# A decode step with attention and a gated FFN: activations as the stationary operand in q projection and FFN up, and w_down in 112 rows

## The chip, the cores and the metric

The kernel runs on one core of a Trainium2 chip. The time is the device time of one execution in microseconds (us). Before the change the runs took 125.03 us in the median (three runs, 124.83 to 125.47). The chip's matrix engine is called PE (its weight loads PEld), the vector engine DVE, the scalar engine ACT, the general engine POOL, and the engine that issues most transfers SP. On PE one operand is loaded first and stays (stationary), the other streams past it (moving).

## The reference, cut to what matters

One token for each of 8 sequences, model width 512, all data bf16.

```python
x  = A_x                                    # 8 x 1 x 512
xn = layernorm(x)
q  = (xn @ wq)                              # 512 x 4096: 32 heads of 128
k, v = last 1024 positions of the caches    # 8 sequences x 8 kv heads x 1024 x 128
o  = softmax(q k^T / sqrt(128)) v           # 4 query heads share a kv head
s  = o @ wo                                 # 4096 x 512
h  = gelu(xn @ w_gate) * (xn @ w_up)        # 512 x 1792 each
g  = silu(h @ w_down)                       # 1792 x 512
out = x + s * g
```

About 47 MB are read: 32 MB of caches (16 groups of K and 16 of V, 1 MB each), wq and wo with 4 MB each, and the three FFN weights with 1.8 MB each. Little is computed per byte.

## The kernel before

**Loads.** Every large load goes into a slot of one ring, `ring`, of 22 slots of 128 partitions x 8192 bytes, and all are issued by SP in one order, written out by hand: K group 0, four parts of wq, then K and V groups in turn (`load_cache`, L86), two halves each of w_gate and w_up (L105) and of w_down (L114), and four parts of wo (L132), the last of which is cut in 768 KB and 256 KB. The transfers are spread over 16 DMA engines. SP holds a load back until the load eight places earlier has landed, and, once the ring has gone round, until PE is done with the slot's last content.

**Start.** The layer norm's result `xhat` (8 x 512) is transposed on PE (L230, L234) into `xnT_sb` and, with another order of rows, `xpT_sb`, 128 x 4 x 8 each. `project_q` has wq as the stationary operand: for each of 4 parts and 32 heads, one matmul with 128 x 128 weights and 8 moving columns (L242). The result has head dimension on partitions, as the scores need it, and one cast (L250) brings it to `qT_all`.

**Attention.** A group is 4 sequences of one kv head. Its K comes as 32 blocks of 128 x 128; PE transposes them eight at a time (L262), DVE copies them to SBUF (L266), and they become the stationary operand of the scores (L274). ACT takes the exponential (L284), a matmul with ones and a DVE reduction give the sums (L296, L298), and V blocks are the stationary operand of the values (L309). The main loop runs over 64 such blocks of eight, transposing two blocks ahead of the scores and multiplying values six blocks behind them. PE runs in program order: what waits there holds up what follows.

**FFN and end.** After the loop, `ffn_up` multiplies 128-column pieces of w_gate and w_up (stationary, read with a step of 7 elements) by `xpT_sb` (8 moving columns, L379): 112 matmuls into one PSUM tile `gu_ps`, with the hidden dimension on partitions. Then come the gelu and the product on ACT and DVE (L389 to L402, 112 elements per partition), which leave `hT_sb`. Between, `select_out` (L350) finishes the rearrangement of the last attention outputs. `ffn_down` (L409) has 8 columns of `hT_sb` stationary and w_down moving, 128 columns at a time, and puts the four quarters of the output at partitions 0, 32, 64 and 96. `project_out` (L363) does the same with wo, part by part as it lands, and two DVE operations and four small stores end the kernel.

```python
load_k(0)
load_wq()
for g in range(1, NG):
    load_k(g)
    load_v(g - 1)
load_v(NG - 1)
load_ffn()
```

Of the kernel before, what the change touches and what calls it, by code (L numbers as in the profile page):

```python
# [8 lines left out]
ALU = mybir.AluOpType  # L9
AX = mybir.AxisListType  # L10
BF16 = mybir.dt.bfloat16
FP32 = mybir.dt.float32
# [3 lines left out]
def kernel(  # L16
# [13 lines left out]
    nc = tc.nc  # L30

    B, Sq, D = A_x.shape
    Hkv, Sk, Dh = A_k_cache.shape[1], A_k_cache.shape[2], A_k_cache.shape[3]
    Hq = A_wq.shape[1] // Dh
    rep = Hq // Hkv
    W = min(4096, max(256, Sk // 4))
    win0 = Sk - W
    F = B_w_gate.shape[1]
    P = nc.NUM_PARTITIONS
    NDC = D // P  # L40
# [11 lines left out]
    NB = C // CB  # L52
    SLOT = C * Dh

    JF = F // 2 // P
    NQ = D // P

    consts = ctx.enter_context(tc.tile_pool(name="consts", bufs=1))
    persist = ctx.enter_context(tc.tile_pool(name="persist", bufs=1))
    ring = ctx.enter_context(tc.tile_pool(name="ring", bufs=22))  # L60
    kT_pool = ctx.enter_context(tc.tile_pool(name="kT_pool", bufs=4))
    p_pool = ctx.enter_context(tc.tile_pool(name="p_pool", bufs=3))
    small = ctx.enter_context(tc.tile_pool(name="small", bufs=3))
# [2 lines left out]
    ps_m = ctx.enter_context(tc.tile_pool(name="ps_m", bufs=2, space=bass.MemoryType.PSUM))  # L66
# [9 lines left out]
    def slot():  # L76
        return ring.tile([P, SLOT], BF16, name="slot")

    k_t, v_t, wo_t = {}, {}, {}
    wq_t, wg_t, wu_t, wd_t = [], [], [], []  # L80
# [20 lines left out]
    def load_ffn():  # L101
        for dst, src in ((wg_t, B_w_gate), (wu_t, B_w_up)):
            for a in range(2):
                t = slot()
                nc.sync.dma_start(  # L105
                    out=t[:, 0 : 2 * F],
                    in_=src[a * 2 * P : (a + 1) * 2 * P, :].rearrange(
                        "(p k) f -> p (k f)", k=2
                    ),
                )  # L110
                dst.append(t[:, 0 : 2 * F].rearrange("p (k f) -> p k f", k=2))
        for a in range(2):
            t = slot()
            nc.sync.dma_start(  # L114
                out=t[:, 0 : JF * D],
                in_=B_w_down[a * JF * P : (a + 1) * JF * P, :].rearrange(
                    "(p j) d -> p (j d)", j=JF
                ),
            )
            wd_t.append(t[:, 0 : JF * D].rearrange("p (j d) -> p j d", j=JF))  # L120


    HS = SLOT // D
# [13 lines left out]
# [5 lines that stand above are left out]
    for m in range(NM):  # L142
        load_wo(m, cut=HS if m < NM - 1 else HS - 2)


    ident = consts.tile([P, P], BF16, name="ident")
    nc.vector.memset(ident, 0.0)
    nc.gpsimd.affine_select(
        out=ident, in_=ident, compare_op=ALU.not_equal, fill=1.0, base=0,
# [10 lines left out]
        out=sel, in_=sel, compare_op=ALU.not_equal, fill=1.0, base=0,  # L160
# [4 lines left out]
        out=diag, in_=sel.rearrange("p r i -> p i r"), axis=AX.X, op=ALU.add  # L165
    )
    nc.vector.tensor_scalar(
        out=diag, in0=diag, scalar1=1.0, scalar2=30000.0, op0=ALU.subtract, op1=ALU.mult
# [6 lines left out]
        out=hmask, in_=hmask, compare_op=ALU.is_ge, fill=0.0, base=0,  # L175
# [3 lines left out]
        out=hmask, in_=hmask, compare_op=ALU.is_ge, fill=0.0, base=B - 1,  # L179
# [5 lines left out]
        out=bsel3, in_=bsel3, compare_op=ALU.not_equal, fill=1.0, base=0,  # L185
# [4 lines left out]
        out=bsel_f, in_=bsel3.rearrange("p h b -> p b h"), axis=AX.X, op=ALU.add  # L190
# [6 lines left out]
    nc.gpsimd.memset(xq_sb, 0.0)  # L197
    for q in range(NQ):
        nc.scalar.dma_start(
            out=xq_sb[32 * q : 32 * q + B, :], in_=x_flat[:, q * P : (q + 1) * P]  # L200
# [12 lines left out]
        out=xhat, in0=x_sb, scalar1=mv[:, 0:1], scalar2=rstd[:, 0:1],  # L213
        op0=ALU.subtract, op1=ALU.mult,
    )

    xnT_sb = persist.tile([P, NDC, B], BF16, name="xnT_sb")
    xpT_sb = persist.tile([P, NDC, B], BF16, name="xpT_sb")
    qT_all = persist.tile([P, Hkv, B, rep], BF16, name="qT_all")
    oT_all = persist.tile([P, Hq, B], BF16, name="oT_all")  # L220
    hT_sb = persist.tile([P, 2 * JF, B], BF16, name="hT_sb")
    g_sb = persist.tile([P, P], FP32, name="g_sb")

    s_ps = ps_s.tile([P, P], FP32, name="s_ps")
# [2 lines left out]
    def transpose_x():  # L227
        t = ps_m.tile([P, 2, NDC, B], BF16, name="m_ps")
        for k in range(NDC):
            nc.tensor.transpose(t[:, 0, k, :], xhat[:, k * P : (k + 1) * P], ident[0:B, 0:B])  # L230
        xp = xhat.rearrange("b (a p k) -> b a k p", a=2, k=2)
        for a in range(2):
            for k in range(2):
                nc.tensor.transpose(t[:, 1, 2 * a + k, :], xp[:, a, k, :], ident[0:B, 0:B])  # L234
        nc.vector.tensor_copy(out=xnT_sb, in_=t[:, 0])
        nc.vector.tensor_copy(out=xpT_sb, in_=t[:, 1])

    def project_q():
        q_ps = ps_m.tile([P, Hq, B], FP32, name="m_ps")
        for k in range(NDC):  # L240
            for h in range(Hq):
                nc.tensor.matmul(  # L242
                    q_ps[:, h, :],
                    wq_t[k][:, h * Dh : (h + 1) * Dh],
                    xnT_sb[:, k, :],
                    start=(k == 0 and h == 0),
                    stop=(k == NDC - 1),
                    skip_group_check=True,
                )
        nc.vector.tensor_copy(  # L250
            out=qT_all, in_=q_ps.rearrange("p (h j) b -> p h b j", j=rep)
        )


    kT, sc, pT, oT = {}, {}, {}, {}
# [104 lines left out]
    def project_out(m):  # L360
        for e in range(HS):
            for q in range(NQ):
                nc.tensor.matmul(  # L363
# [7 lines left out]


    def ffn_up():
        gu_ps = ps_m.tile([P, 2, 2 * JF, B], FP32, name="m_ps")
        for w, wt in enumerate((wg_t, wu_t)):
            for j in range(2 * JF):
                f0 = (j // JF) * (F // 2) + j % JF
                for k in range(NDC):
                    nc.tensor.matmul(  # L379
                        gu_ps[:, w, j, :],  # L380
                        wt[k // 2][:, k % 2, f0 : f0 + (P - 1) * JF + 1 : JF],
                        xpT_sb[:, k, :],
                        start=(k == 0),
                        stop=(k == NDC - 1),
                    )
        shape = [P, 2 * JF, B]
        zT, uT = gu_ps[:, 0], gu_ps[:, 1]
        z2 = persist.tile(shape, FP32, name="z2")
        nc.scalar.activation(out=z2, in_=zT, func=ACT.Square)  # L389
        nc.vector.tensor_scalar(  # L390
            out=z2, in0=z2, scalar1=0.044715, scalar2=1.0, op0=ALU.mult, op1=ALU.add
        )
        u3 = persist.tile(shape, FP32, name="u3")
        nc.vector.tensor_tensor(out=u3, in0=z2, in1=zT, op=ALU.mult)
        th = persist.tile(shape, FP32, name="th")
        nc.scalar.activation(out=th, in_=u3, func=ACT.Tanh, scale=0.7978845608028654)
        nc.vector.tensor_scalar(
            out=th, in0=th, scalar1=0.5, scalar2=0.5, op0=ALU.mult, op1=ALU.add
        )
        gz = persist.tile(shape, FP32, name="gz")  # L400
        nc.vector.tensor_tensor(out=gz, in0=th, in1=zT, op=ALU.mult)
        nc.vector.tensor_tensor(out=hT_sb, in0=gz, in1=uT, op=ALU.mult)  # L402

    def ffn_down():
        f_ps = ps_m.tile([P, P], FP32, name="m_ps")
        nc.vector.memset(f_ps, 0.0)
        for j in range(2 * JF):
            for q in range(NQ):
                nc.tensor.matmul(  # L409
                    f_ps[32 * q : 32 * q + B, :],  # L410
                    hT_sb[:, j, :],
                    wd_t[j // JF][:, j % JF, q * P : (q + 1) * P],
                    start=(j == 0),
                    stop=(j == 2 * JF - 1),
                    skip_group_check=True,
                )
        th2 = persist.tile([P, P], FP32, name="th2")
        nc.scalar.activation(out=th2, in_=f_ps, func=ACT.Tanh, scale=0.5)
        nc.vector.tensor_scalar(
            out=th2, in0=th2, scalar1=0.5, scalar2=0.5, op0=ALU.mult, op1=ALU.add  # L420
        )
        nc.vector.tensor_tensor(out=g_sb, in0=th2, in1=f_ps, op=ALU.mult)


    LA, LAG = 2, 6
    N = NG * NB
    transpose_x()
    for n in range(LA):
        transpose_block(n)
    project_q()  # L430
    for n in range(N + LAG):
        if n + LA < N:
# [3 lines left out]
        if n >= LAG:  # L436
# [3 lines left out]
            if g % GM == 0 and g > 0:  # L440
                if s == 0:
                    expand_out(g // GM - 1)
                if s == 3:
                    select_out(g // GM - 1)
    expand_out(NM - 1)
    ffn_up()
    select_out(NM - 1)
    ffn_down()
# [8 lines left out]
    nc.vector.tensor_tensor(out=out_sb, in0=tmp, in1=xr_sb, op=ALU.add)  # L457
    for q in range(NQ):
        eng = nc.sync if q % 2 == 0 else nc.scalar
        eng.dma_start(  # L460
            out=out_flat[:, q * P : (q + 1) * P], in_=out_sb[32 * q : 32 * q + B, :]
# [31 lines left out]
```

## Time and profile before

| what | value |
|---|---|
| median of the runs | 125.03 us |
| profiled execution, its own time | 124.83 us |
| its span in the profile | 123.1 us |
| PE, PEld busy | 85.5, 79.9 us |
| DVE, ACT, POOL busy | 69.1, 22.0, 2.1 us |
| read from HBM | 47.46 MB, 386 GB/s over the span |
| q projection: matmuls L242 | 128, 4.1 us |
| FFN up: matmuls L379 | 112, 6.5 us |
| FFN down: matmuls L409 | 56, 1.7 us |
| transposes of K, L262 | 512, 45.5 us |

A line of the profile names the source line, the engine, the operation, output and inputs with their shapes, how often it ran and how long. In square brackets or behind a bar stands how long the engine was idle before, and what it waited for. The slices divide the span into 40 equal parts of about 3.1 us; a digit is the busy share in tenths. PEclk is the share of full clock that PE was granted: 0.50 in some stretches, 1.00 in others. The chain that ended last is followed back from the last instruction. The times in a timeline count from the start of the span.

### The profile page before, as it was taken

The numbers are of one execution on the slowest core, as the hardware profiler recorded it, in microseconds if no ns is written. First come the engines' busy times: TensorE is split into PE (matmuls) and PEld (weight loads), VectorE is DVE, ScalarE is ACT, GpSimd is POOL, SyncE is SP. The second block draws the span as 40 slices with busy tenths as digits, with TensorE's granted clock in tenths as the row PEclk, the third lists the DMA queues.
The fourth block names the chain that finished last, engine by engine and source line by source line (L and its number), as shares of the span: only waits on it lengthen the run. The fifth ranks groups of instructions, "written<-read, shape, count | busy, mean of one in ns | idle before, by whom it ended". The sixth has DMA issues, their size and how long they took to land.

```text
span 123.1 us, 4441 instructions
## 1 busy us (share of the span) xinstructions
PE 85.5 (69%) x2020; PEld 79.9 (65%) x2020; DVE 69.1 (56%) x146; ACT 22.0 (18%) x70; POOL 2.1 (2%) x13
## 2 busy tenths in 40 slices
PE   0075339696976968999987982998799756927260
PEld 0075339595865947999976982998699646926240
DVE  2352006775956849579997990769899660052001
ACT  0440000330303302121330330123033300010000
POOL 6000000000000000000000000000000000000000
PEclk9999999999999975559999997569999965556955
DMA  3999999999999999999999999999999999999820
GB/s 88 397 415 434 418 415 423 423 413 421 410 418 415 418 418 413 423 410 421 413 413 418 423 418 418 423 407 415 407 423 410 422 415 412 413 417 426 322 106 5
DMA packets 6931, 47.76 MB, mean 388 GB/s; under 512 B 888, under 2 KB 896, under 8 KB 1920
## 3 DMA queue, kind: packets, MB, share of 16 engines
q1 hardware_dynamic: 6800, 47.46, 93.7%
q8 instruction: 16, 0.26, 0.9%
q10 hardware_dynamic: 112, 0.02, 0.1%
q14 instruction: 3, 0.02, 0.0%
HBM read 47.46 MB, written 0.01 MB: 386 GB/s over the span
## 4 chain that ended last, share of the span: by engine, by line
DMA 88%; PE 5%; SPq 3%; issue 1%; DVE 0%
DMA slot<-in_A_k_cache_dram 50%; DMA slot<-in_B_w_gate_dram 16%; DMA slot<-in_A_wo_dram 15%; DMA slot<-in_A_wq_dram 7%; SPq L86 3%; PE kT_ps L262 3%; PE s_ps L363 1%; PE m_ps L309 1%; PE sc_ps L274 0%; SPq L98 0%; PE m_ps L296 0%; DVE tmp L455 0%; DVE out_sb L457 0%; SPq L132 0%
## 5 line engine op out<-in xcount | busy, mean ns | idle before, releaser
L266 DVE COPY kT<-kT_ps 128x1024 bf16<-128x1024 bf16 x64 | 42.3, 678 | 19.1 <-PE kT_ps L262 18.4
L262 PE MATMUL kT_ps<-ident,slot 128*128 128x128 bf16 x512 | 45.5, 241 | 9.9 <-DMA slot<-in_A_k_cache_dram 9.8
L262 PEld LDWEIGHTS <-slot 128*128 128x128 bf16 x512 | 34.3, 108 | 13.4 <-DMA slot<-in_A_k_cache_dram 10.6
L284 ACT ACTIVATE pT<-sc_ps,diag 128x128 bf16<-128x128 f32 x64 | 18.3, 368 | 71.6 <-PE sc_ps L274 71.6
L274 PE MATMUL sc_ps<-qT_all,kT 128*128 128x16 bf16 x512 | 23.0, 172 | 0.0
L309 PE MATMUL m_ps<-pT,slot 128*128 128x16 bf16 x512 | 21.8, 170 | 0.2 <-issue 0.2
L309 PEld LDWEIGHTS <-slot 128*128 128x128 bf16 x512 | 18.6, 97 | 3.5 <-issue 2.0
L274 PEld LDWEIGHTS <-kT 128*128 128x128 bf16 x512 | 20.8, 100 | 0.0
L298 DVE TENSOR_REDUCE sums<-m_ps 128x16 f32<-128x512 f32 x16 | 10.9, 683 | 1.0 <-PE m_ps L296 1.0
L242 PE MATMUL m_ps<-xnT_sb,slot 128*128 128x8 bf16 x128 | 4.1, 169 | 5.5 <-DMA slot<-in_A_wq_dram 5.5
L379 PE MATMUL m_ps<-xpT_sb,slot 128*128 128x8 bf16 x112 | 6.5, 195 | 2.0 <-DMA slot<-in_B_w_up_dram 1.3
L379 PEld LDWEIGHTS <-slot 128*128 128x128 bf16 x112 | 6.2, 153 | 2.3 <-DMA slot<-in_B_w_up_dram 1.3
L242 PEld LDWEIGHTS <-slot 128*128 128x128 bf16 x128 | 3.9, 105 | 5.7 <-DMA slot<-in_A_wq_dram 5.7
L296 PE MATMUL m_ps<-pT,ones_pp 128*128 128x512 bf16 x16 | 6.7, 416 | 0.7 <-ACT pT L284 0.7
L250 DVE CAST qT_all<-m_ps 128x256 bf16<-128x256 f32 x1 | 0.4, 425 | 8.6 <-PE m_ps L242 8.6
L336 DVE TENSOR_TENSOR wide<-m_ps,hmask 64x1024 bf16<-64x1024 bf16 x4 | 4.9, 1217 | 0.4 <-PE m_ps L332 0.3
L230 PE MATMUL m_ps<-ident,xhat 8*128 8x8 bf16 x4 | 0.3, 168 | 6.9 <-DVE xhat L212 6.9
L230 PEld LDWEIGHTS <-xhat 8*128 8x128 bf16 x4 | 0.2, 104 | 6.9 <-DVE xhat L212 6.9
L390 DVE TENSOR_SCALAR z_2490<-z_2490 128x112 f32<-128x112 f32 x1 | 0.2, 219 | 7.5 <-ACT z_2490 L389 7.5
L302 DVE RECIPROCAL recip<-sums 128x16 f32<-128x16 f32 x16 | 4.0, 253 | 0.5
L455 DVE TENSOR_TENSOR tmp<-s_ps,g_sb 128x128 f32<-128x128 f32 x1 | 0.3, 292 | 6.5 <-PE s_ps L363 6.5
L318 DVE TENSOR_TENSOR oT_all<-m_ps,recip 128x16 bf16<-128x16 f32 x16 | 3.5, 218 | 0.3
(63 smaller groups left out, 28.4 us busy)
## 6 DMA issues: line engine op xcount, KB each, us to landing
slot<-in_A_k_cache_dram SPq DMA_DIRECT2D x16, 1024.0 KB, 19.9
slot<-in_A_v_cache_dram SPq DMA_DIRECT2D x16, 1024.0 KB, 19.9
slot<-in_A_wq_dram SPq DMA_DIRECT2D x4, 1024.0 KB, 8.7
slot<-in_A_wo_dram SPq DMA_DIRECT2D x3, 1024.0 KB, 18.4
slot<-in_B_w_gate_dram SPq DMA_DIRECT2D x2, 896.0 KB, 19.4
slot<-in_B_w_up_dram SPq DMA_DIRECT2D x2, 896.0 KB, 19.0
slot<-in_B_w_down_dram SPq DMA_DIRECT2D x2, 896.0 KB
slot<-in_A_wo_dram SPq DMA_DIRECT2D x1, 768.0 KB, 18.1
```

The costliest lines, as they stand in the source:

```text
L86: nc.sync.dma_start(out=t, in_=rows)
L242: nc.tensor.matmul(q_ps[:, h, :], wq_t[k][:, h * Dh : (h + 1) * Dh], xnT_sb[:, k, :], start=(k == 0 and h == 0), stop=(k == NDC - 1), skip ...
L262: nc.tensor.transpose(t_ps[:, c * P : (c + 1) * P], k_t[g][:, cc * Dh : (cc + 1) * Dh], ident)
L266: nc.vector.tensor_copy(out=kT[n], in_=t_ps)
L274: nc.tensor.matmul(sc[g][:, s * CB + c, :], kT[n][:, c * P : (c + 1) * P], qT_all[:, hkv, b0 : b0 + I, :], start=True, stop=True,)
L284: nc.scalar.activation(out=pT[g][:, :, i * rep : (i + 1) * rep], in_=sc[g][:, :, i * rep : (i + 1) * rep], func=ACT.Exp, bias=diag[:, i : ...
L296: nc.tensor.matmul(sums_ps, ones_pp, pT[g], start=True, stop=True)
L298: nc.vector.tensor_reduce(out=sums, in_=sums_ps.rearrange("p c m -> p m c"), axis=AX.X, op=ALU.add)
L302: nc.vector.reciprocal(out=recip[g], in_=sums)
L309: nc.tensor.matmul(oT[g], v_t[g][:, c * Dh : (c + 1) * Dh], pT[g][:, c, :], start=(c == 0), stop=(c == C - 1),)
L336: nc.vector.tensor_tensor(out=wide, in0=t_ps.rearrange("p (q e) -> p e q", e=HS) .unsqueeze(2) .to_broadcast([HS * B, HS, HS, DQ]), in1=hm ...
L379: nc.tensor.matmul(gu_ps[:, w, j, :], wt[k // 2][:, k % 2, f0 : f0 + (P - 1) * JF + 1 : JF], xpT_sb[:, k, :], start=(k == 0), stop=(k == N ...
```

## The change

Four things change together.

The activations become the stationary operand of the q projection and of FFN up, padded to 32 columns (`xnT_sb` and `xpT_sb` grow to 128 x 4 x 32, zeroed by POOL), and the weights move past them: 512 columns of wq at a time, 448 of w_gate and w_up, the latter with a step of 8 elements. Four such matmuls write to partitions 0, 32, 64 and 96 of one PSUM tile. There are 32 matmuls instead of 128 and 32 instead of 112.

The results then have the sequences on partitions, so they are copied to SBUF and transposed on PE: 8 transposes and four DVE copies for q (in place of one cast), 4 transposes and one copy for the FFN's hidden values. The gelu works on 448 elements per partition instead of 112, and its gate half and up half now lie in separate PSUM tiles.

The hidden dimension is cut in 16 pieces of 112 rows instead of 14 of 128. w_down is loaded in two transfers of 112 partitions x 8192 bytes instead of 128 x 7168, and `ffn_down` does 64 matmuls instead of 56.

The ring has 21 slots instead of 22. The order of the loads is the same; K group 0 is one transfer in both kernels.

```diff
-    JF = F // 2 // P
+    FP = F // 16
+    JF = F // 2 // FP
+    JH = JF // 2
     NQ = D // P
+    Q = 32
-    ring = ctx.enter_context(tc.tile_pool(name="ring", bufs=22))
+    ring = ctx.enter_context(tc.tile_pool(name="ring", bufs=21))
...
-                out=t[:, 0 : JF * D],
-                in_=B_w_down[a * JF * P : (a + 1) * JF * P, :].rearrange(
+                out=t[0:FP, :],
+                in_=B_w_down[a * JF * FP : (a + 1) * JF * FP, :].rearrange(
                     "(p j) d -> p (j d)", j=JF
...
-    xnT_sb = persist.tile([P, NDC, B], BF16, name="xnT_sb")
-    xpT_sb = persist.tile([P, NDC, B], BF16, name="xpT_sb")
+    xnT_sb = persist.tile([P, NDC, Q], BF16, name="xnT_sb")
+    xpT_sb = persist.tile([P, NDC, Q], BF16, name="xpT_sb")
+    nc.gpsimd.memset(xnT_sb, 0.0)
+    nc.gpsimd.memset(xpT_sb, 0.0)
-    hT_sb = persist.tile([P, 2 * JF, B], BF16, name="hT_sb")
+    hT_sb = persist.tile([FP, JH, P], BF16, name="hT_sb")
...
     def project_q():
-        q_ps = ps_m.tile([P, Hq, B], FP32, name="m_ps")
+        NW = rep * Dh
+        q_sb = persist.tile([P, Hkv // NQ, NW], BF16, name="q_sb")
+        q_ps = [ps_m.tile([P, NW], FP32, name="m_ps") for n in range(Hkv // NQ)]
         for k in range(NDC):
-            for h in range(Hq):
+            for hkv in range(Hkv):
+                n, q = hkv // NQ, hkv % NQ
                 nc.tensor.matmul(
-                    q_ps[:, h, :],
-                    wq_t[k][:, h * Dh : (h + 1) * Dh],
+                    q_ps[n][Q * q : Q * (q + 1), :],
                     xnT_sb[:, k, :],
+                    wq_t[k][:, hkv * NW : (hkv + 1) * NW],
...
-        nc.vector.tensor_copy(
-            out=qT_all, in_=q_ps.rearrange("p (h j) b -> p h b j", j=rep)
-        )
+        for n in range(Hkv // NQ):
+            nc.vector.tensor_copy(out=q_sb[:, n, :], in_=q_ps[n])
+        t_ps = ps_m.tile([P, Hkv // NQ, rep, NQ, Q], BF16, name="m_ps")
+        for n in range(Hkv // NQ):
+            for j in range(rep):
+                nc.tensor.transpose(
+                    t_ps[:, n, j].rearrange("p q r -> p (q r)"),
+                    q_sb[:, n, j * Dh : (j + 1) * Dh],
+                    ident,
+                )
+        for n in range(Hkv // NQ):
+            nc.vector.tensor_copy(
+                out=qT_all[:, n * NQ : (n + 1) * NQ],
+                in_=t_ps[:, n, :, :, 0:B].rearrange("p j q b -> p q b j"),
+            )
...
     def ffn_up():
-        gu_ps = ps_m.tile([P, 2, 2 * JF, B], FP32, name="m_ps")
+        gu_ps = [ps_m.tile([P, JH * FP], FP32, name="m_ps") for w in range(2)]
         for w, wt in enumerate((wg_t, wu_t)):
-            for j in range(2 * JF):
-                f0 = (j // JF) * (F // 2) + j % JF
-                for k in range(NDC):
+            for k in range(NDC):
+                for q in range(NQ):
+                    a, j0 = q // 2, JH * (q % 2)
+                    cols = wt[k // 2][:, k % 2, a * JF * FP : (a + 1) * JF * FP]
                     nc.tensor.matmul(
-                        gu_ps[:, w, j, :],
-                        wt[k // 2][:, k % 2, f0 : f0 + (P - 1) * JF + 1 : JF],
+                        gu_ps[w][Q * q : Q * (q + 1), :],
                         xpT_sb[:, k, :],
+                        cols.rearrange("x (p j) -> x j p", j=JF)[:, j0 : j0 + JH, :],
...
-        nc.vector.tensor_tensor(out=hT_sb, in0=gz, in1=uT, op=ALU.mult)
+        h_sb = persist.tile(shape, BF16, name="h_sb")
+        nc.vector.tensor_tensor(out=h_sb, in0=gz, in1=uT, op=ALU.mult)
+        h_ps = ps_m.tile([FP, JH, P], BF16, name="m_ps")
+        for c in range(JH):
+            nc.tensor.transpose(h_ps[:, c, :], h_sb[:, c * FP : (c + 1) * FP], ident)
+        nc.vector.tensor_copy(out=hT_sb, in_=h_ps)
...
         for j in range(2 * JF):
+            r, c = j // JH, j % JH
             for q in range(NQ):
                 nc.tensor.matmul(
-                    f_ps[32 * q : 32 * q + B, :],
-                    hT_sb[:, j, :],
+                    f_ps[Q * q : Q * q + B, :],
+                    hT_sb[:, c, Q * r : Q * r + B],
```

More of the change, by code (lines that the diff above doesn't have):

```diff
@@ L119, in load_ffn @@
             )
-            wd_t.append(t[:, 0 : JF * D].rearrange("p (j d) -> p j d", j=JF))
+            wd_t.append(t[0:FP, :].rearrange("p (j d) -> p j d", j=JF))
     HS = SLOT // D
@@ L234, in transpose_x @@
                 nc.tensor.transpose(t[:, 1, 2 * a + k, :], xp[:, a, k, :], ident[0:B, 0:B])
-        nc.vector.tensor_copy(out=xnT_sb, in_=t[:, 0])
-        nc.vector.tensor_copy(out=xpT_sb, in_=t[:, 1])
+        nc.vector.tensor_copy(out=xnT_sb[:, :, 0:B], in_=t[:, 0])
+        nc.vector.tensor_copy(out=xpT_sb[:, :, 0:B], in_=t[:, 1])
     def project_q():
-        q_ps = ps_m.tile([P, Hq, B], FP32, name="m_ps")
+        NW = rep * Dh
+        q_sb = persist.tile([P, Hkv // NQ, NW], BF16, name="q_sb")
+        q_ps = [ps_m.tile([P, NW], FP32, name="m_ps") for n in range(Hkv // NQ)]
         for k in range(NDC):
-            for h in range(Hq):
+            for hkv in range(Hkv):
+                n, q = hkv // NQ, hkv % NQ
                 nc.tensor.matmul(
-                    q_ps[:, h, :],
-                    wq_t[k][:, h * Dh : (h + 1) * Dh],
+                    q_ps[n][Q * q : Q * (q + 1), :],
                     xnT_sb[:, k, :],
-                    start=(k == 0 and h == 0),
+                    wq_t[k][:, hkv * NW : (hkv + 1) * NW],
+                    start=(k == 0),
                     stop=(k == NDC - 1),
@@ L373, in ffn_up @@
     def ffn_up():
-        gu_ps = ps_m.tile([P, 2, 2 * JF, B], FP32, name="m_ps")
+        gu_ps = [ps_m.tile([P, JH * FP], FP32, name="m_ps") for w in range(2)]
         for w, wt in enumerate((wg_t, wu_t)):
-            for j in range(2 * JF):
-                f0 = (j // JF) * (F // 2) + j % JF
-                for k in range(NDC):
+            for k in range(NDC):
+                for q in range(NQ):
+                    a, j0 = q // 2, JH * (q % 2)
+                    cols = wt[k // 2][:, k % 2, a * JF * FP : (a + 1) * JF * FP]
                     nc.tensor.matmul(
-                        gu_ps[:, w, j, :],
-                        wt[k // 2][:, k % 2, f0 : f0 + (P - 1) * JF + 1 : JF],
+                        gu_ps[w][Q * q : Q * (q + 1), :],
                         xpT_sb[:, k, :],
+                        cols.rearrange("x (p j) -> x j p", j=JF)[:, j0 : j0 + JH, :],
                         start=(k == 0),
                         stop=(k == NDC - 1),
+                        skip_group_check=True,
                     )
-        shape = [P, 2 * JF, B]
-        zT, uT = gu_ps[:, 0], gu_ps[:, 1]
+        shape = [P, JH * FP]
+        zT, uT = gu_ps
         z2 = persist.tile(shape, FP32, name="z2")
```

## The prediction

> **What bounds the kernel now.** I read the page's slices first, then the chain that ended last in order of time, then the timeline of the end, then stretches of one microsecond.
>
> ```profile
> DMA  3999999999999999999999999999999999999820
> GB/s 88 397 415 434 418 415 423 423 413 421 410 418 415 418 418 413 423 410 421 413 413 418 423 418 418 423 407 415 407 423 410 422 415 412 413 417 426 322 106 5
> q1 hardware_dynamic: 6800, 47.46, 93.7%
> q8 instruction: 16, 0.26, 0.9%
> DMA 88%; PE 5%; SPq 3%; issue 1%; DVE 0%
> ```
>
> The 16 DMA engines run without a gap at about 418 GB/s from 3 us on, and 88% of the chain is transfers. So bytes and rate set the time; PE (85.5 of 123.1 us busy) doesn't. The second queue, 16 packets of 16 KB, matters below.
>
> ```profile
> 81.21 19.29 DMA slot<-in_B_w_gate_dram
> ...
> 100.56 18.12 DMA slot<-in_A_wo_dram
> 118.68 0.04 issue
> 118.72 1.07 PE s_ps L363 x32
> 119.78 0.02 issue
> 119.81 0.30 DVE tmp L455
> 120.11 0.02 issue
> 120.13 0.29 DVE out_sb L457
> ```
>
> The last large weight piece lands at 118.68; after it come 32 matmuls, two vector operations and the store. Anything done before 118.68 is free if PE is there in time.
>
> ```profile
> 111.93 1.07 PE L363 MATMUL s_ps<-slot,oE_1142 128*8 128x128 bf16 x32
> 114.30 0.62 PE L363 MATMUL s_ps<-slot,oE_1645 128*8 128x128 bf16 x32 [1.30 <-DMA slot<-in_A_wo_dram]
> 116.81 1.03 PE L363 MATMUL s_ps<-slot,oE_2148 128*8 128x128 bf16 x32 [1.89 <-DMA slot<-in_A_wo_dram]
> 118.72 1.04 PE L363 MATMUL s_ps<-slot,oE_2510 128*8 128x128 bf16 x32 [0.88 <-DMA slot<-in_A_wo_dram]
> ```
>
> PE waits 1.30 + 1.89 + 0.88 = 4.1 us for wo pieces after the FFN, so the FFN has about 4 us of slack. The lines also price column tiles: 32 matmuls of 128 columns in four tiles take 0.62 us at full clock, 19 ns each (77 ns per group of four), and 1.04 us at half clock (130 ns per group).
>
> ```profile
> 115.00:116.00 1.00, 0.00 (x0) 0.00 (x0) 0.00 (x0) 0.00 (x0) 0.00 (x0) 1.00 0.84 326
> 116.00:117.00 1.00, 0.19 (x12) 0.19 (x15) 0.00 (x0) 0.00 (x0) 0.00 (x0) 0.79 0.52 211
> 117.00:118.00 1.00, 0.84 (x32) 0.64 (x25) 0.00 (x0) 0.00 (x0) 0.00 (x0) 0.50 0.47 195
> 118.00:119.00 1.00, 0.28 (x14) 0.28 (x17) 0.00 (x0) 0.00 (x0) 0.00 (x0) 0.50 0.31 115
> ```
>
> The last two numbers are DMA share and GB/s. The engines do not end together: from 115 on they drop out, and the rest work to the end. The landing records (one per engine and load) say the same: the sixteen parts of a wq load arrive within 0.4 us, those of the last 768 KB piece at 115.43 (first) to 118.68 (last), seven of them over 3 us behind. The steps are about 1.6 us each and follow the 16 KB instruction packets: each delays one engine, eight engines take turns, and those with two packets are the 3.2 us late ones. **A load lands with its slowest engine.**
>
> [...] about 4040 PE rows, 16 packets. [...] a packet of 8192 bytes takes 0.313 us, 26.2 GB/s. All large loads of this kernel have 128 rows, so no row here shows 112.
>
> **The change, part by part.**
>
> *q projection.* Before: the last wq part lands at 17.46, 32 matmuls take 1.02 us, one cast 0.43, the first score is at 19.04, 1.6 us after the landing. After, for that part: two groups of four matmuls of 512 columns, 4 x 77 = 0.31 us each. The cast of half 0 can start after the first (0.31); then two casts of 128x512 from PSUM (nearest: the reduction L298 of that size, 683 ns) 1.37; four transposes (eight of L262 take 0.61) 0.3 plus 0.2 for the last to drain; a copy of 128 elements 0.2 (L358: 203 to 225 ns); five handovers of 0.06 to 0.1, 0.35. Sum 2.7 us, so scores start about 1.1 us later. If the four tiles didn't overlap, each matmul would take the 0.22 us from the start of L296 to the next, eight 1.7 us, and the delay would be about 2.5. Behind these instructions on PE stand the transposes of K blocks from the third on, and their copies on DVE; nothing of the DMA: SP's loads do not wait on PE before the ring has gone round, at the 22nd load (about 39.7 us). PE then has 1.35 us idle at 24.8 and 1.2 in each 5 us after, so it is back within two groups. Cost 0; without that cover 1.1 to 2.5. The two POOL memsets (L197: 0.2 us each) end near 3.7, and their readers come at 7.36: 0.
>
> *FFN up.* Before: the second half of w_up is there at 104.94, 54 matmuls take 3.0 us, the gelu chain and waits 2.5, down starts at 110.48 and ends at 112.15. After: 8 matmuls of 448 columns, two groups, half clock: 2 x 3.5 x 130 ns = 0.9 us (with no overlap, at twice 0.22 us and 448/512, 3.1; the moving rows are read with a step of 16 bytes, which no row shows: doubling gives 1.8). The gate half of the gelu runs while w_up arrives; what is left is one product of 128x448, 0.7 us (112 elements 0.27, 128 elements of L455 0.29), four transposes at half clock 0.5, a copy of 512 columns 0.37, then select_out, which now waits for a PSUM buffer of ffn_up, its copy, the memset and handovers, 1.1. Down starts near 108.5, and has 64 instead of 56 matmuls at 30 ns, 1.9 us: 110.4, 1.7 us earlier. With no overlap it is 112.6, still under the 114.30 at which PE goes on. Gain or loss at the end: 0.
>
> *Ring of 21.* A load waits for the PE work on the load 21 before, not 22, i.e. 2.5 us earlier. SP's order is the same, and each load already waits for the landing of the eighth before it (20 us in flight); the slot before was landed some 32 us earlier. 0.
>
> *PE instructions.* 4042 to 3730 rows, 312 fewer, so 14 packets instead of 15 before the last data. Engines with two packets remain, since that is more than eight. Gain 0; it would need another deal of packets to engines to gain up to 1.6.
>
> *w_down in 112 rows of 8192 bytes, not 128 of 7168.* Same bytes, twice 0.92 MB, same bytes per engine (7 x 8192 = 8 x 7168). [...] 7 x 0.313 = 2.19 us per load against 8 x 0.275 = 2.20: 0. [...] The late engines have no reserve, and the two loads stand ahead of wo in every engine's queue, so it goes straight to the end. I take +2.5. What is late next: wo, then the last 32 matmuls.
>
> *Sum.* Span 123.1 + 2.5 = 125.6; the profiled execution took 124.83, 1.7 more than its span, so 127.3; the median of the runs is 0.2 above it: **127.5**.
>
> **Rivals.** (1) *Rows land at full rate whatever their partitions.* Then all parts are hidden and nothing moves: 125.0, from 124.5 to 125.5. [...] It decides if a w_down packet of 8192 bytes stays near 0.31 us; this case ends not slower. [...] (3) *Something gains:* the last matmuls at full clock end at best 0.2 earlier, because the final 256 KB land at 119.33; packets dealt otherwise take off up to 1.6; 123.5 to 124.4. Against: eight turns are seen twice over. (4) *PE becomes the end:* tiles that don't overlap, with doubled reads, make each group of eight 6 us, FFN up 99.5 + 24 = 123.5, and the end about 10 us later, 135. Against: 19 ns per matmul of 128 columns in L363 can't be without overlap.
>
> **How the numbers follow.** [...] No cost: 0.23. Gain: 0.06. Worse than +5 by either road: 0.05. About 0.5% is what a measurement of this kernel can tell from no change. Faster 0.07 (gain and the edge of no cost), same 0.28, slower 0.65. Range 124.7 to 130.0, which leaves out the gain, the worst and the lowest edge of no cost.
>
> **What would show it.** Right: w_down packets of 8192 bytes well over 0.31 us, a dip under 400 GB/s between 96 and 112 us (slices 32 to 37), the final wo landing near 121, q's first score near 20, PE still waiting for wo after an earlier ffn_down. Wrong: GB/s flat at 418 and the last landing at 118.7; or PE busy without a DMA wait at the end.

## The result, and the profile after

The changed kernel takes 129.93 us in the median (129.61 to 130.94) beside 124.97 for the kernel before: a ratio of 1.040, with a 95% interval of 1.034 to 1.047. It is 5.0 us slower. The forecast was 2.5 slower, at 127.5; the direction and the place were right and the size was half. The profiled execution took 130.14 us, with a span of 128.1.

From the page of the changed kernel, the transfers by slice and the two queues:

```profile
DMA  3999999999999999999999999999999999999820
GB/s 120 397 427 412 438 420 438 415 430 422 425 425 417 427 420 435 415 430 420 425 427 417 435 412 432 412 438 417 421 428 422 282 197 220 207 287 436 360 97 5
...
q1 hardware_dynamic: 6768, 47.46, 94.0%
q8 instruction: 14, 0.23, 0.7%
```

For 31 slices the rate is as before or a little higher. Then it falls to about half for five slices (197 to 287 GB/s) while the row above stays at 9: the engines are all busy and move about half as much. There are 14 instruction packets instead of 16.

Stretches of two microseconds over that dip; the last two numbers are DMA share and GB/s:

```profile
98.00:100.00 2.00, 1.91 (x12) 0.70 (x16) 1.25 (x2) 0.00 (x0) 0.00 (x0) 0.50 1.03 432
100.00:102.00 2.00, 2.00 (x16) 0.41 (x12) 0.00 (x0) 0.00 (x0) 0.00 (x0) 0.77 1.15 258
102.00:104.00 2.00, 1.65 (x9) 0.12 (x1) 1.02 (x2) 0.76 (x2) 0.00 (x0) 1.00 1.03 189
...
108.00:110.00 2.00, 1.28 (x16) 0.75 (x12) 0.79 (x2) 0.00 (x0) 0.00 (x0) 0.50 1.06 229
...
114.00:116.00 2.00, 1.02 (x32) 0.83 (x32) 0.00 (x0) 0.20 (x1) 0.00 (x0) 0.50 0.97 401
```

A share of 1.0 at 190 to 260 GB/s means that a packet takes about twice as long, not that engines stand idle. The packet records of the trace agree: from 96 us to the end 378 packets took more than 1.3 times their usual duration (327 of 8192 bytes, 49 of 7168 and two of 6144), most of the 8192-byte ones near 0.6 us instead of 0.31. w_down has 224 packets, all of 8192 bytes. So at least 154 of the slow packets belong to other loads: those of 7168 bytes to w_gate or w_up, and at least 103 of the others to wo. What the slow packets took beyond the usual, added up and divided by the 16 engines, is 7.2 us.

The chain that ended last, its end in order of time:

```profile
...
98.74 24.89 DMA slot<-in_A_wo_dram
123.63 0.04 issue
123.68 1.05 PE s_ps L385 x31
...
```

It still ends with the last large piece of wo and 1.05 us of matmuls; the landing has moved from 118.68 to 123.63. The parts of that piece arrive from 120.35 (first engine) to 123.63 (last), before from 115.43 to 118.68: every engine is 4.9 us later, and the spread of 3.3 us is the same.

PE at the end, from the timeline:

```profile
98.34 5.31 PE L402 MATMUL m_ps<-slot,xpT_sb 128*32 128x448 bf16 x24
106.63 1.77 PE L402 MATMUL m_ps<-slot,xpT_sb 128*32 128x448 bf16 x8 [2.99 <-DMA slot<-in_B_w_up_dram]
...
114.73 1.02 PE L439 MATMUL m_ps<-slot,hT_sb 112*8 112x128 bf16 x32 [2.83 <-DMA slot<-in_B_w_down_dram]
116.98 1.02 PE L385 MATMUL s_ps<-slot,oE_1062 128*8 128x128 bf16 x32 [1.23 <-DMA slot<-in_A_wo_dram]
119.42 1.02 PE L385 MATMUL s_ps<-slot,oE_1565 128*8 128x128 bf16 x32 [1.41 <-DMA slot<-in_A_wo_dram]
121.85 1.03 PE L385 MATMUL s_ps<-slot,oE_2068 128*8 128x128 bf16 x32 [1.41 <-DMA slot<-in_A_wo_dram]
123.68 1.03 PE L385 MATMUL s_ps<-slot,oE_2358 128*8 128x128 bf16 x32 [0.80 <-DMA slot<-in_A_wo_dram]
```

PE waits for w_down (2.83 us) and then for each part of wo, as before: nothing on PE sets the end.

One thing was not forecast. Up to the first half of w_gate the changed kernel runs ahead: the first engine's part of it is there at 93.49 instead of 95.07. From about 4 us up to there a packet of 8192 bytes takes 309 ns almost without exception; in the kernel before it took 313 (most), 316 or 320 from about 12 us on. So the 5.0 us are a loss of nearly 7 less a gain of nearly 2, and both needed an explanation.

### The profile page after: what moved, and what is told of

The parts are those of the page before. It is cut to its first block, busy times and chain, and to the rows that moved or that the text cites. A ratio compares the mean times of both kernels' runs of the same rounds, so it can differ in the third digit from the quotient of the medians.

```text
span 128.1 us, 4139 instructions
## 1 busy us (share of the span) xinstructions
PE 88.0 (69%) x1864; PEld 72.9 (57%) x1864; DVE 72.0 (56%) x150; ACT 22.6 (18%) x70; POOL 2.4 (2%) x15
## 4 chain that ended last, share of the span: by engine, by line
DMA 95%; PE 1%; SPq 1%; DVE 0%; issue 0%
DMA slot<-in_A_k_cache_dram 56%; DMA slot<-in_A_wo_dram 19%; DMA slot<-in_B_w_gate_dram 15%; DMA slot<-in_A_wq_dram 5%; PE s_ps L385 1%; SPq L90 1%; DVE tmp L485 0%; DVE out_sb L487 0%; SPq L136 0%; SPq L109 0%
## 5 line engine op out<-in xcount | busy, mean ns | idle before, releaser
L284 PE MATMUL kT_ps<-ident,slot 128*128 128x128 bf16 x512 | 44.5, 238 | 9.9 <-DMA slot<-in_A_k_cache_dram 9.6
L284 PEld LDWEIGHTS <-slot 128*128 128x128 bf16 x512 | 33.5, 106 | 13.5 <-DMA slot<-in_A_k_cache_dram 10.3
L331 PEld LDWEIGHTS <-slot 128*128 128x128 bf16 x512 | 18.5, 97 | 3.4 <-issue 1.9
L402 PE MATMUL m_ps<-slot,xpT_sb 128*32 128x448 bf16 x32 | 7.1, 971 | 3.0 <-DMA slot<-in_B_w_up_dram 3.0
L252 PE MATMUL m_ps<-slot,xnT_sb 128*32 128x512 bf16 x32 | 4.2, 618 | 3.5 <-DMA slot<-in_A_wq_dram 3.5
L402 PEld LDWEIGHTS <-xpT_sb 128*32 128x32 bf16 x32 | 1.2, 106 | 7.3 <-issue 5.9
L261 DVE CAST q_sb<-m_ps 128x512 bf16<-128x512 f32 x2 | 1.3, 686 | 6.5 <-PE m_ps L252 6.5
L439 PE MATMUL m_ps<-slot,hT_sb 112*8 112x128 bf16 x64 | 2.1, 307 | 3.6 <-DMA slot<-in_B_w_down_dram 3.6
L252 PEld LDWEIGHTS <-xnT_sb 128*32 128x32 bf16 x32 | 1.0, 110 | 6.0 <-issue 5.8
L439 PEld LDWEIGHTS <-hT_sb 112*8 112x8 bf16 x64 | 1.6, 119 | 3.9 <-issue 3.0
```

What stands on the lines that cost most here:

```text
L252: nc.tensor.matmul(q_ps[n][Q * q : Q * (q + 1), :], xnT_sb[:, k, :], wq_t[k][:, hkv * NW : (hkv + 1) * NW], start=(k == 0), stop=(k == NDC ...
L284: nc.tensor.transpose(t_ps[:, c * P : (c + 1) * P], k_t[g][:, cc * Dh : (cc + 1) * Dh], ident)
L331: nc.tensor.matmul(oT[g], v_t[g][:, c * Dh : (c + 1) * Dh], pT[g][:, c, :], start=(c == 0), stop=(c == C - 1),)
L402: nc.tensor.matmul(gu_ps[w][Q * q : Q * (q + 1), :], xpT_sb[:, k, :], cols.rearrange("x (p j) -> x j p", j=JF)[:, j0 : j0 + JH, :], start= ...
L439: nc.tensor.matmul(f_ps[Q * q : Q * q + B, :], hT_sb[:, c, Q * r : Q * r + B], wd_t[j // JF][:, j % JF, q * P : (q + 1) * P], start=(j == ...
```

## The experiments

All were timed against the kernel before on the same chip, where it took 124.94 to 124.98 us.

**The kernel before again.** Unchanged, to see whether 309 against 313 ns is the chip.

> The kernel before, unchanged, for its profile on the same chip as the experiments. In the changed kernel a 1 MB load took 2.45 us per engine where the kernel before took 2.49, and the V loads had landed 1.6 us earlier. If that is the chip, this profile shows 2.45 too (span about 121.5); if it is the change, 2.49 and a span near 123.1.

Measured: 124.86 us, span 123.2, packets again at 313 to 320 ns after the first 12 us. It is the kernel, not the chip.

**w_down back in 128 rows, the rest of the change kept.**

```diff
-                out=t[0:FP, :],
-                in_=B_w_down[a * JF * FP : (a + 1) * JF * FP, :].rearrange(
-                    "(p j) d -> p (j d)", j=JF
+                out=t[:, 0 : 7 * D],
+                in_=B_w_down[a * 7 * P : (a + 1) * 7 * P, :].rearrange(
+                    "(p j) d -> p (j d)", j=7
...
```

> The changed kernel with w_down loaded as 128 rows of 7168 bytes, as before; FFN down then multiplies only rows 0 to 111 of each block, so its output is not the reference's. Theory ([...]the rest of the change is hidden): 124.5 to 125.2, no packet over 0.4 us besides those beside an instruction fetch, GB/s flat. Rival (part of the 5 us is on PE, in the strided FFN or the longer q chain): 126.5 or more with GB/s flat. Rival (the ring of 21): stays near 130.

Measured: 123.15 us, ratio 0.986 (0.982 to 0.989), under the range expected. Its span and its rates:

```profile
span 121.0 us, 4139 instructions
...
GB/s 114 395 420 412 425 431 433 422 428 425 417 425 422 428 425 425 420 425 425 420 428 422 430 420 425 417 425 425 428 425 423 415 419 437 420 425 424 338 85 5
```

The dip is gone, with only three packets over 1.3 times their usual duration after 96 us. So w_down's 112 rows cost 129.93 - 123.15 = 6.8 us, and all the rest of the change together gains 1.8 us. The q projection, FFN up and FFN down cost nothing that shows at the end, but "the rest of the change is hidden" was wrong too: something in it gains.

**w_down in 112 rows alone, in the kernel before.**

```diff
-                out=t[:, 0 : JF * D],
-                in_=B_w_down[a * JF * P : (a + 1) * JF * P, :].rearrange(
-                    "(p j) d -> p (j d)", j=JF
+                out=t[0:112, :],
+                in_=B_w_down[a * 896 : (a + 1) * 896, :].rearrange(
+                    "(p j) d -> p (j d)", j=8
...
```

> The kernel before with w_down alone loaded as 112 rows of 8192 bytes; FFN down multiplies only rows 0 to 111, so its output is not the reference's. Theory: 129.5 to 132, with packets of 0.6 us and about 200 GB/s for some 13 us. Rival (the loss needs the new PE work beside it): near 125.

Measured: 132.42 us, ratio 1.060 (1.056 to 1.063), slightly over the range.

```profile
span 130.7 us, 4441 instructions
...
GB/s 90 404 424 426 419 414 426 409 426 409 424 411 424 409 416 414 421 416 416 411 421 416 419 416 419 414 409 424 409 418 413 255 174 223 211 293 421 343 101 5
```

The same dip, 7.5 us of loss, without any of the new work on PE beside it. The form of this load is enough by itself.

**One of the two loads in 112 rows.** The first half of w_down in 112 rows, the second in 128.

> The changed kernel with the first half of w_down in 112 rows and the second in 128; the second half is multiplied with rows 0 to 111 alone, so its output is not the reference's. Theory: half the loss, 127 to 128, low GB/s for half the time. If a meeting of two such loads is what costs: 125.5 to 126.5. If one such load already sets the engines apart for good: near 129.

Measured: 128.22 us, 1.025 (1.020 to 1.029).

```profile
span 126.0 us, 4139 instructions
...
GB/s 83 411 421 424 434 427 424 421 434 414 421 434 421 416 429 432 414 427 424 432 411 427 429 429 414 432 421 427 417 424 430 389 197 220 255 432 422 347 81 5
```

The loss against 128 rows for both is 5.1 us, more than half of 6.8. One load costs three quarters of what two cost; so the loss is not a fixed sum per load. The median fits none of the three expectations exactly (it is 0.2 over the first). The trace has 267 slow packets here, more than twice the 112 that the one load of 112 rows has, and 378 with two such loads; why the second adds so little was not tried.

**128 rows of 8192 bytes.** This keeps the length of the rows and the 16 pieces, and loads 16 rows too many.

```diff
-                out=t[0:FP, :],
-                in_=B_w_down[a * JF * FP : (a + 1) * JF * FP, :].rearrange(
+                out=t,
+                in_=B_w_down[a * 6 * P : (a * 6 + 8) * P, :].rearrange(
```

> The changed kernel with w_down loaded in 128 rows of 8192 bytes, that is 16 rows of eight more than needed per load (rows 0 to 1023 and 768 to 1791; FFN down multiplies rows 0 to 111 of each, the second from the wrong place, so its output is not the reference's). 262144 bytes more to move, 0.6 us at the 26.5 GB/s of 16 engines. Theory (the number of partitions decides): 123.6 to 124.0 with packets at 309 ns, 6 us less than with 112 rows although it loads more. Rival (rows of 8192 bytes in w_down, or 16 pieces in FFN down, cost): 129 or more.

Measured: 123.74 us (ratio 0.990, 0.988 to 0.992), 0.6 above the version with 128 rows of 7168, as the 262144 bytes more ask for. After 96 us four packets are slow, not 378. More bytes over all 128 partitions are 6.2 us faster than fewer bytes over 112.

**The same rows in two halves of 64 partitions**, in the kernel before. This tests a load over part of the partitions without the number 112.

```diff
-            nc.sync.dma_start(
-                out=t[:, 0 : JF * D],
-                in_=B_w_down[a * JF * P : (a + 1) * JF * P, :].rearrange(
...
+            src = B_w_down[a * JF * P : (a + 1) * JF * P, :].rearrange(
+                "(p j) d -> p (j d)", j=JF
+            )
+            for lo in (0, 64):
+                nc.sync.dma_start(out=t[lo : lo + 64, 0 : JF * D], in_=src[lo : lo + 64, :])
```

> The kernel before with each w_down load cut in two transfers of 64 partitions, 0 to 63 and 64 to 127: same rows, same bytes[...]. Theory[...]: packets of 7168 bytes at about 0.55 us instead of 0.28, about half of 418 GB/s while they run, time 129 to 133. Rival (what costs is that 112 is not a power of two, or seven rows per engine): 124.6 to 125.4.

Measured: 131.80 us, 1.053 (1.050 to 1.056).

```profile
span 129.8 us, 4443 instructions
...
GB/s 106 411 411 437 409 429 414 416 424 406 424 419 416 419 404 427 406 429 406 421 416 411 421 414 419 419 404 429 412 417 411 294 225 247 208 278 428 320 93 5
```

About half the rate again, for about five slices; 307 packets of 7168 bytes are slow, 0.50 us in the median where the usual is 0.275. 64 is a power of two, and here as with 112 rows each transfer has sixteen landing records, so all engines take part; the rival of the number 112 is out. What the two slow forms share is that each of their transfers covers fewer than 128 partitions. So it is shown that the spread of a load over the partitions costs the time, and not shown why: which engine wrote which partition is not in the trace, and a reason on the side of the memory that is read was not tested.

**The same 112 rows at other times.** w_down goes into tiles of its own, right behind wq, and in another run behind V group 7, the eighth (the second diff).

```diff
-    ring = ctx.enter_context(tc.tile_pool(name="ring", bufs=21))
+    ring = ctx.enter_context(tc.tile_pool(name="ring", bufs=19))
...
+    def load_down():
         for a in range(2):
-            t = slot()
+            t = persist.tile([P, SLOT], BF16, name=f"down{a}")
...
     load_k(0)
     load_wq()
+    load_down()
```

```diff
...
         load_v(g - 1)
+        if g == 8:
+            load_down()
     load_v(NG - 1)
```

> The changed kernel with the two w_down loads of 112 rows moved right behind wq, into tiles of their own (19 slots in the ring), at a time when the engines are within 0.4 us of each other instead of 3.2 apart. Theory A (the setting apart of the engines by instruction packets[...]): loss clearly smaller than late in the kernel, time 125 to 127.5 against 129.9. Theory B (the loss is a matter of the rows alone): 129.5 to 130.5.

> As the run with w_down's 112 rows right behind wq, but loaded after the seventh V group, at some 45 to 60 us, when one round of instruction packets has set about half of the engines 1.6 us behind. Early, with the engines together, the loss against 128 rows was 2.0 us; at the end, 3.2 us apart, 6.8. Theory (the loss grows with how far the engines are apart): a loss of 3.5 to 5.5, time 126.6 to 128.6. Rival (only the start of the kernel is cheap, for another reason): near 129.9; or only its end is dear: near 125.1.

Measured: 125.12 us early and 127.86 in the middle. Early, then middle:

```profile
span 123.0 us, 4138 instructions
...
GB/s 85 421 424 424 421 301 296 384 426 426 426 424 424 426 424 424 421 429 421 429 418 426 418 434 421 424 421 426 424 429 426 415 433 416 427 425 419 360 101 5
```

```profile
span 125.7 us, 4138 instructions
...
GB/s 86 412 422 430 428 420 425 428 433 415 420 430 433 415 417 430 428 331 222 242 289 425 438 415 428 417 438 412 422 425 435 412 426 425 432 418 417 357 89 5
```

Against 123.15 with 128 rows the loss is 2.0 us early, 4.7 in the middle and 6.8 at the end. By the landing records ahead of the first slow packets, the engines are then 0.4, 1.9 and 3.0 us apart. The distance comes with the packets of instructions: in the kernel before, the first of them starts at 15.3 us and takes 1.06, and of the wq part that lands next, at 17.41, one of the 16 records is 1.8 us behind the first and none of the others more than 0.3. The loss grows with this distance. The distance was varied through the place in the kernel alone, so another cause that grows with time isn't excluded.

How far the slow packets account for the loss can be summed from the traces. The excess is what they took beyond the usual (309, 272 and 234 ns by size, and 313, 275 and 238 in the kernel before), divided by the 16 engines:

| run | slow packets | excess | loss measured |
|---|---|---|---|
| two loads of 112 rows, early | 207 | 2.0 us | 2.0 us |
| two, in the middle | 302 | 4.6 us | 4.7 us |
| two, at the end | 378 | 7.2 us | 6.8 us |
| one, at the end | 267 | 4.7 us | 5.1 us |
| two in halves of 64, kernel before | 422 | 6.7 us | 6.8 us |

So within some tenths the loss is these packets and nothing else.

**Where the 1.8 us come from.** The built programs show where the slots of the ring lie: from byte 25568 of each partition in the kernel before, from 35072 in the changed one. 35072 is 137 x 256; 25568 is 224 over a multiple of 256. The 9504 bytes between them are the new and larger tiles ahead of the ring (`q_sb` 2048, `h_sb` 896, four FFN tiles 5376 more, `hT_sb` 800 more, `xnT_sb` and `xpT_sb` 384 more). They moved the ring, by chance, to a multiple of 256; the number of its slots does not move its start. Two runs test it: the kernel before with a spare tile of 32 bytes ahead of the ring, and the changed kernel with w_down in 128 rows, shifted by 224 bytes (112 columns in the spare tile instead of 16).

```diff
+    pad = consts.tile([P, 16], BF16, name="pad")
+    nc.vector.memset(pad, 0.0)
     ident = consts.tile([P, P], BF16, name="ident")
```

> The kernel before with an unused tile of 32 bytes ahead of the ring, so that the slots begin on a multiple of 256 bytes in each partition (25600 instead of 25568). In the changed kernel the slots begin at 35072, also a multiple of 256, and packets of 8192 bytes take 309 ns where before they take 313 to 320. Theory (the start of the slots is the 1.8 us that the rest of the change gained): 123.0 to 123.4, packets at 309. Rivals (the new q projection or FFN, fewer instruction packets, or 21 slots instead of 22): 124.6 to 125.2, packets at 313 to 320.

> The changed kernel with w_down in 128 rows of 7168 bytes (FFN down multiplies rows 0 to 111 alone, so its output is not the reference's) and an unused tile of 224 bytes ahead of the ring, so that the slots begin at 35296, 224 over a multiple of 256, as in the kernel before. Theory (the start of the slots): back to 124.6 to 125.2, packets at 313 to 320. Rivals (q projection, FFN, instruction packets, number of slots): stays at 123.1.

Measured: 122.93 us for the first (0.984, 0.981 to 0.986) and 124.85 for the second (0.998, 0.997 to 1.000). The kernel before, aligned, then the changed one, shifted:

```profile
span 121.0 us, 4442 instructions
...
GB/s 106 390 417 433 428 417 428 428 412 431 425 431 422 422 422 414 433 420 428 420 431 425 417 428 422 431 412 436 425 420 416 424 422 424 429 430 416 339 104 5
```

```profile
span 123.1 us, 4140 instructions
...
GB/s 67 405 428 429 423 423 426 418 415 410 413 423 413 418 418 421 415 413 410 421 413 423 426 413 421 407 410 415 421 426 406 422 413 417 411 421 424 321 88 5
```

The packets follow: 309 ns throughout in the first, 313 to 320 in the second after its first 12 us. 32 bytes of padding are worth 2.0 us, and the shift takes the gain away. The rest of the change shows no part in it, the ring of 21 included (the first run has 22 slots and gains, the second 21 and does not): with equal alignment the two kernels are within about 0.2 us of each other in both pairs (122.93 and 123.15; 124.97 and 124.85). The shifted start costs 1.3 to 3.6% on a packet of 8192 bytes (313 to 320 ns beside 309). Why it does is not shown, nor why most packets of the first 12 us of the kernel before, into slots with the same offset, took 309 ns. Only two offsets were run, 0 and 224 bytes over a multiple of 256; whether a smaller multiple would do as well is not known.

**A whole version.** The changed q projection, FFN up with contiguous moving columns, w_down in 128 rows, slots on a multiple of 256. Each of the four column tiles takes 448 neighbouring columns, and the hidden values get back to 128 partitions by transposes to either half:

```diff
...
-                    cols = wt[k // 2][:, k % 2, a * JF * FP : (a + 1) * JF * FP]
...
-                        cols.rearrange("x (p j) -> x j p", j=JF)[:, j0 : j0 + JH, :],
+                        wt[k // 2][:, k % 2, q * FQ : (q + 1) * FQ],
...
+        for lo in (0, H):
+            for j in range(JF):
+                nc.tensor.transpose(h_ps[lo : lo + H, j, :], hc[:, j, :], ident)
...
```

> A whole version: the changed q projection, FFN up with the 448 moving columns contiguous, 14 transposes of 64 columns each to the lower or upper half of the partitions, so that the hidden values lie as in the kernel before, w_down in 128 rows of 7168 bytes, 56 matmuls in FFN down, and the slots on a multiple of 256 bytes. Theory: 123.0 to 123.4, as with w_down in 128 rows alone, since transfers set the end; the groups of four matmuls of FFN up fall from 0.89 us to about 0.45 if the step of 16 bytes in the moving read is what doubled them. Rival (the strided read was hidden cost): below 122.9.

Measured: 122.81 us (122.81 to 122.89), 0.983 of the kernel before (0.981 to 0.985). PE's timeline at the end:

```profile
103.06 0.94 PE L402 MATMUL m_ps<-slot,xpT_sb 128*32 128x448 bf16 x8 [1.17 <-DMA slot<-in_B_w_up_dram]
...
107.09 1.66 PE L443 MATMUL m_ps<-slot,hT_sb 128*8 128x128 bf16 x56 [0.67 <-DVE m_ps L440]
...
116.61 1.02 PE L387 MATMUL s_ps<-slot,oE 128*8 128x128 bf16 x32 [0.87 <-DMA slot<-in_A_wo_dram]
```

A group of four matmuls of 448 contiguous columns takes 0.94 / 2 = 0.47 us, at a PEclk of 0.50. With the step of 16 bytes it took 5.31 / 6 = 0.89 from 98.34 on and 1.77 / 2 = 0.89 at 106.63. PEclk was 0.50 until 100.9 us and 1.00 from there to 107.7, and the strided groups start about 0.8 us apart at either clock. So at half clock the step doubles the group, and the full clock did not make the strided group faster.

FFN down is done at 108.75, and the end waits for wo (0.87 us). The time, 122.81, falls in the range of the rival that the strided read was a hidden cost. But it is only 0.1 under the kernel before with 32 bytes of padding, inside the intervals, and the profiled spans of this run, of that one and of the changed kernel with w_down in 128 rows are all 121.0 us; so no cost of the strided read is shown. The whole version is as fast as the padded kernel, and both beat the two kernels.

## Why the prediction was right and wrong

- **Which part decides: right.** w_down's form was put on the path, all else at nothing. With w_down's rows undone 1.8 us of gain are left, and these belong to the address of the ring, not to the work on PE.
- **What w_down's rows do: right in what was seen, not shown in its cause.** Foreseen were packets of 8192 bytes well over 0.31 us and a dip to under 400 GB/s between 96 and 112 us; the profile has packets of about 0.6 us and 190 to 260 GB/s from 100 to 114. The halves of 64 partitions behave alike: 0.50 us in the median where 0.275 is usual. Why such rows are slow no run shows.
- **The size of w_down's term: wrong, and this is the step that failed.** The +2.5 was my estimate, and nothing in the trace of the kernel before could bear it out, because no load there has 112 rows. Measured were 6.8. The estimate slowed only w_down's own rows, and took all engines to run in step. With the engines 0.4 us apart, early in the kernel, the two loads cost 2.0 us. At the end they are 3.0 us apart. That is longer than one such load should take (an estimate: seven packets of the 0.313 us measured before, 2.19), so some engines should be writing w_down while others write w_up or wo. Other loads do pay: 378 packets were slow, and w_down has only 224. That it is the distance between the engines that makes the rows dearer is argued from three places in the kernel, and was not tested by itself.
- **The start of the ring, not priced at all: wrong.** For the ring I asked only which load waits for which slot; 0 for that was right. That the new tiles move the ring's start, and that this changes each packet, I did not look at. It hid 1.8 of the 6.8 us.
- **Instruction packets: right.** 14 in place of 16, eight engines take turns (after twelve packets, four of the sixteen parts of w_gate's second half land 3.0 us behind the first and four 1.4 to 1.6), and the last piece's spread is 3.3 us as before.
- **q projection: right on the outcome, short in the sum.** From the landing of the last wq part to the first score's weights it took 18.84 - 15.64 = 3.2 us; worked out were 2.7. PE was slower there than the prices I took: eight matmuls took 1.04 us, not 0.62, and eight transposes of K took 1.01 us at 21.34 and 0.61 at 22.41. That is the ratio of half clock, though the PEclk row reads 1.00; its first record in this trace is at 22.4 us. It cost nothing even at that point: the last wq part came 1.8 us earlier, because the first instruction packet fell at 23.1 instead of 15.3, and scores started at 18.84 beside 19.04. The score "near 20" that I named as a sign did not come.
- **FFN up: right on the outcome, with the doubt confirmed.** The strided moving read made the group of four 0.89 us, twice the contiguous one at half clock. The last two groups took the 1.8 us that doubling at half clock gives, but mostly at full clock, so that agreement is in part luck. The four tiles do overlap: at 106.63 four matmuls start within 0.01 us of each other, each of 0.95, and the next four 0.77 us later.
- **The rivals.** Rows at full rate are ruled out by the dip and the 6.8 us. PE as the end is ruled out by the waits for wo (0.80 us before the last group). Something did gain, but by neither of the roads that I named.

## What to carry to other kernels

In a kernel that is bound by transfers, the first thing to read in a change is the form of its transfers: how many partitions they cover and at which byte they begin, before any count of matmuls. Here the loads over all 128 partitions were the fast ones, even with useless rows in them (0.6 us for those, against 6.8 for 112 rows). Look too at which byte the tiles of a load begin, because a few bytes of another tile can move them: here 32 bytes of padding took the ring from 224 bytes over a multiple of 256 to a multiple, and 2.0 us off the time. And when a price rests on engines that run in step, look whether they do; the landing records of the kernel before already showed 3.2 us between them.

## What the runs showed of the hardware that I had not expected

- 32 bytes of padding ahead of the ring: 124.98 to 122.93 us. Packets of 8192 bytes fell from 313 to 320 ns to 309, of 7168 from 275 to 282 to 272, of 6144 from 238 to 245 to 234.
- The same two loads of 112 rows cost 2.0, 4.7 and 6.8 us according to where in the kernel they stand.
- One such load at the end costs 5.1 us, two cost 6.8; with one, 267 packets were slow, with two 378.
- The group of four strided matmuls took 0.89 us at half clock and no less at full clock; contiguous at half clock it took 0.47.
